# Second network in scaled float16 pairs, with its partial sums kept in three PSUM banks

## The chip, the cores and the metric

The kernel runs on one core of one Trainium2 chip. The metric is the device time of the program in microseconds, taken as the median of three runs of it. The profile is of one execution of the same program.

## What is computed

Three stages follow each other. First comes an attention over 2 x 8 heads, 768 positions and 64 values per head, in which each query sees only the keys that fall into the same hash bucket (six sign bits). Its output is laid out as 1536 tokens of 512 values. The first network and the second network then work on the tokens:

```python
def _moe_ref(x, w_in, w_out):            # 512 -> 2048 -> 512
    h = x @ w_in
    g = h - np.tanh(h)
    return (g @ w_out).astype(np.float32)

def _moe2_ref(x, domain_probs, w1, w2):  # 4 experts, 512 -> 1024 -> 512
    p = domain_probs / (domain_probs.sum(-1, keepdims=True) + 1e-09)
    out = np.zeros((N, D), dtype=np.float32)
    for e in range(E):
        h = np.maximum(x @ w1[e], 0.0)
        out += p[:, e:e + 1] * (h @ w2[e])
    return out.astype(np.float32)
```

The weights of the first network come in as float64, all the rest as float32.

## The kernel before

All work is put down as a list of operations (`Plan.add`, line 130), each with a priority, the engines that may do it with a planned cost, what it reads and writes, and the buffers that it uses. `Plan.order` (line 155) then plays this list through on the planned costs. At each moment it takes, for each free engine, the operation with the lowest sum of priority and planned wait, and gives out buffers as they come free. The order that results is the order in which every engine, and SP's queue of DMA issues, gets its instructions. Nothing is reordered later: an instruction that waits holds up what stands behind it on its engine. A class of buffers may receive its members late in the plan (`gives_later`, `hand`), when what used the same memory has been planned.

Precision is kept by pairs: an operand is written as a high part and the remainder, and a product is made by three matmuls, high by high, high by remainder and remainder by high. In the attention the pairs are float16. In both networks they are float32r.

*First network.* The tokens are worked on in three blocks (c = 0, 1, 2) of 512. `network_up` (line 804) makes 16 blocks of hidden units, `network_down` (line 822) adds them into four banks of PSUM. At the end four copies on ScalarE (line 1118) put a block's result, transposed, back into `xs[c]`. For block 2 these copies wait until everything that batch 0 still reads from the old buffers is done (`sums[0]`).

*Between the networks.* The second network uses Strassen's scheme in Winograd's form: seven products in place of eight. The tokens make two batches (b = 0, 1) of 768, and each is cut into halves of 384 tokens and halves of the 512 inputs. `moving(b)` (line 860) makes seven operands for the batch, three of them halves of the input themselves, four of them differences, and cuts each into a pair: the high part on ScalarE (line 322), the remainder on VectorE or GpSimd (line 325). `moving(0)` has a priority of 540, `moving(1)` of 734; the down groups of block 2 have 580 to 730.

*Second network.* There are 16 blocks u of hidden units (4 experts, 4 blocks of 256 units each). `stationary(u)` (line 913) loads the weights, makes four sums of quarters of the first matrix (line 927, VectorE or GpSimd), and cuts seven stationary operands and the rows of the second matrix into pairs. `step2(u, b)` (line 945) is one step. It has seven products of six matmuls of 384 columns (line 958), each into a bank of its own. Seven additions on VectorE (`plus`, line 969) and one copy on ScalarE combine them into four results of the hidden layer. `hidden` makes a pair of each: a relu on ScalarE (line 978) and the remainder on VectorE (line 979). Then come six groups, one for each 128 tokens, of six matmuls of 512 columns (`down3`, line 1013), the down groups. VectorE multiplies each by the expert's weight and adds it to the output in `xs` (lines 1021 and 1023). Two banks serve the down groups and six the products. The priorities run 20 units per step, and the down groups of a step lie beside the products of the next. The first writing of the output (u = 0) waits until both batches are cut, since the output takes the place of the cut tokens.

The last step's outputs go to HBM from SP's queue.

Of the kernel before, what the change touches and what calls it, by code (L numbers as in the profile page):

```python
# [16 lines left out]
P = 128  # L17
# [31 lines left out]
NST = 3  # L49
NRQ = 2  # L50
# [31 lines left out]


class Same(Slot):
    def __init__(self, of):
        super().__init__()
        self.of = of

    @property
    def tile(self):  # L90
        return self.of.tile

    @tile.setter
    def tile(self, t):
        pass
# [150 lines left out]
def attn_moe_kernel(ctx: ExitStack, tc: tile.TileContext, qk, v, proj, ident, wa, wb, dp, out):  # L246
# [34 lines left out]
    xs = [xo.tile([P, 4, DM], F32, tag="xo", name=f"xs{c}") for c in range(NC)]  # L281

# [576 lines left out]

    def moving(b, p):  # L860

        bo = [("bo%d" % b, o) for o in range(7)]

        def xat(kh, c, a, n):
            return xs[c][:, 2 * kh : 2 * kh + 2, a : a + n]

        def x2(kh, *cs):
            return [("x2", c, db) for c in cs for db in (2 * kh, 2 * kh + 1)]

        def cut_(o, src, i, j, r, use, p):  # L870

            n = 2 * (j - i)
            hi, lo = (lambda: pl[bo[o]][:, :, 0, i:j]), (lambda: pl[bo[o]][:, :, 1, i:j])
            h32 = lambda: hi().bitcast(F32)
            k = ("part", *bo[o], i)
            sums[b].append(add(p, {AC: (0.05 + n * 0.92e-3, act_copy(hi, src))}, r, [(k, "hi")], [bo[o], *use]))
            sums[b].append(both(
                p + 0.1, sub(nc.vector, lo, src, h32), sub(nc.gpsimd, lo, src, h32), n, [*r, (k, "hi")], [(k, "lo")], [bo[o], *use]
            ))
# [33 lines left out]
    def stationary(u, p):  # L913
# [15 lines left out]
        for m, (o, n, src, r) in enumerate((  # L929
# [5 lines left out]
            h32 = lambda hi=hi: hi().bitcast(F32)  # L935
            k = ("parts", u, m)
            use = [ao, *w, *([sx] if m == 2 else [])]
            add(p + 3 + m, {AC: (0.05 + n * 0.19, act_copy(hi, src))}, r, [(k, "hi")], use)
            both(p + 3.1 + m, sub(nc.vector, lo, src, h32), sub(nc.gpsimd, lo, src, h32), 256 * n, [*r, (k, "hi")], [(k, "lo")], use)
        for i in range(2):  # L940
            w2, v_ = ("wr", u, i, 1), ("w2", u, i)
            dma(p + 2, lambda w2=w2: pl[w2], lambda i=i: wb[e * NF2 + 2 * j + i, :, 1], w=[w2], lat=1.1)
            split(p + 8 + i, lambda v_=v_: pl[v_], lambda w2=w2: pl[w2], [w2], ("w2k", u, i), [v_])

    def step2(u, b, p, q):

        e, j = divmod(u, NF2 // 2)
        ch = {o: ("ch", u, b, o) for o in range(7)}
        ao = ("ao", u)
        bank = lambda o: pl[ch[o]][:, 0:HN]  # L950

        def product(pm, a, o):
            def f():
                n = 0
                for k in range(2):
                    hi, lo = (pl[ao][:, a, i, k * P : k * P + P] for i in range(2))
                    for x, i in ((hi, 0), (hi, 1), (lo, 0)):
                        nc.tensor.matmul(bank(o), x, pl["bo%d" % b, o][:, k, i, :], start=(n == 0), stop=(n == 5))  # L958
                        n += 1

            m = (0, 0, 1, 2, 2, 2, 2)[a]
            return add(p + pm, {TE: (1.04, f)}, [(("parts", u, m), i) for i in ("hi", "lo")] + ready_[b][o], [ch[o]], [ao])

        rs = [("rs", u, b, n) for n in range(2)]

        def plus(pm, o, n, to=None):

            dst = (lambda: bank(o)) if to is None else (lambda: pl[rs[to]][:, 0:HN])
            add(p + pm, {VE: (0.465, lambda: nc.vector.tensor_tensor(out=dst(), in0=bank(o), in1=pl[rs[n]][:, 0:HN], op=ALU.add))},  # L969
                [ch[o], rs[n]], [ch[o] if to is None else rs[to]])  # L970
# [4 lines left out]
        def hidden(pm, o, i, s):  # L975
            hi, lo = (lambda x=x: pl[hb[i]][:, x, s * HN : s * HN + HN] for x in range(2))
            k, key = ("hk", u, b, i, s), ch[o]
            add(p + pm, {AC: (0.37, lambda: nc.scalar.activation(hi(), bank(o), AF.Relu))}, [key], [(k, "hi")], [hb[i]])  # L978
            add(p + pm + 0.1, {VE: (0.465, lambda: nc.vector.scalar_tensor_tensor(
                out=lo(), in0=bank(o), scalar=0.0, in1=hi().bitcast(F32), op0=ALU.max, op1=ALU.subtract  # L980
            ))}, [key, (k, "hi")], [(k, "lo")], [hb[i]])
# [7 lines left out]
        product(2, 4, 4)  # L989
        plus(2.5, 4, 0, 0)  # L990
        product(4, 5, 5)
        plus(4.5, 5, 0, 1)
        product(6, 3, 3)
        plus(6.5, 3, 0, 0)
        plus(6.6, 3, 1)
        hidden(6.7, 3, 1, 1)
        product(8, 2, 6)
        plus(8.5, 6, 1)
        hidden(8.6, 6, 1, 0)
        product(10, 6, 2)  # L1000
        plus(10.5, 2, 0)
        hidden(10.6, 2, 0, 1)
        for t in range(2 * HN // P):
# [13 lines left out]
            add(q + (2, 5, 7, 8, 11, 12)[t], {TE: (1.362, down3)},  # L1017
# [8 lines left out]
            add(q + (2, 5, 7, 8, 11, 12)[t] + 0.5, {VE: (0.66, f)}, [dn, ("pw",), ("o", tb)], [("o", tb)], after=sums[0] + sums[1] if u == 0 else ())  # L1026
# [84 lines left out]
    for c in range(NC):  # L1111
# [4 lines left out]
        for db in range(4):  # L1116
# [41 lines left out]
    new = {"fo": NF1 - 3, "fo2": 3, "xp1": KB4, "raw": 2, "wd": 2, "bo0": 2}  # L1158
# [7 lines left out]
    def switch():  # L1166
# [3 lines left out]
        def space(name, words, kind=F32):  # L1170
# [30 lines left out]
    def stationaries():  # L1201
        t = space("fa", 14 * CH, F32R)
        return [part(t, i * 7 * CH, 7 * CH).rearrange("p (o i n) -> p o i n", o=7, i=2) for i in range(2)]

    def hiddens(t, n):
        return [part(t, MV * i, MV).rearrange("p (i n) -> p i n", i=2) for i in range(n)]

    gives_later("bo0", 3, lambda: made["bo0a"], ups1)
    for n in ("rw", "rq"):
        gives_later("bo0", 1, lambda n=n: movers(space(n, 2 * 2 * CH, F32R), 0, 1), raw_)  # L1210
    gives_later("bo1", 4, lambda: movers(space("fb", 13 * CH, F32R), 0, 4), net)
    gives_later("bo1", 1, lambda: movers(space("hp2", 4 * CH, F32R), 0, 1), net)
    gives_later("bo1", 2, lambda: movers(xa_t, 0, 2), ups2)
    gives_later("ao", 2, stationaries, ups2)
    gives_later("sx", 1, lambda: [fa2_t.rearrange("p (o n) -> p o n", o=4)], ups2)
    gives_later("wr", 2, lambda: made["wr"], ups2)
    gives_later("hb", 3, lambda: hiddens(space("tp", NTH * CH, F32R), 3), net)
    gives_later("hb", 1, lambda: hiddens(hp_t, 1), net)
    gives_later("w2", 2, lambda: made["w2"], net)
# [4 lines left out]
    outs2 = those("fo2")  # L1224
    for n in range(3):
        hand("fo2", n, "rs", False, outs2)
    for n in range(2):
        hand("wu", n, "w2", False, ups2)
# [59 lines left out]
```

## Time and profile before

| what | us |
|---|---|
| median of three runs | 983.17 |
| lowest and highest run | 982.15, 983.32 |
| span of the profiled execution | 978.8 |
| TensorE busy | 964.1 |
| VectorE busy | 754.3 |
| ScalarE busy | 438.8 |
| GpSimd busy | 294.2 |

The span reaches from the first to the last instruction of the profiled execution, whose own time is not listed apart from its span; the runs' times hold some microseconds more, outside it. The profile calls TensorE's matmuls PE and its weight loads PEld, VectorE DVE, ScalarE ACT, GpSimd POOL and SyncE SP; line numbers (L958) are those of the kernel before. A tile's name stands for the memory that an operation writes or reads, by the pool that held it first: in the second network `fa` is the stationary operands, `ab`, `fb`, `xa`, `rw`, `rq` and `hp` are operands of the products, and `st`, `sf`, `po` are banks of PSUM. Matmuls are pipelined, so a matmul's own duration is longer than the time from its start to the next one's; prices of matmuls are taken from start to start.

### The profile page before, as it was taken

What the parts mean: (1) busy time and instruction counts of PE and PEld (TensorE: products, weight loads), DVE (VectorE), ACT (ScalarE), POOL (GpSimd) and SP (SyncE); (2) the same over time, 40 slices, a digit from 0 to 9 for tenths busy, and PEclk for the clock granted to TensorE, in tenths of its full rate; (3) what the DMA queues carried; (4) which work ended last, traced back from release to release, by engine and by line L of the source; (5) the groups of instructions that cost most, each with busy time, mean ns of one, the idle gap of its engine ahead of it and who ended that gap; (6) DMA issues with size and microseconds to landing.
All of it is one profiled execution on the core that took longest, in us unless ns stands there. A gap on an engine that the chain in (4) does not pass through costs nothing.

```text
span 978.8 us, 17209 instructions
## 1 busy us (share of the span) xinstructions
PE 964.1 (99%) x6508; PEld 804.3 (82%) x6508; DVE 754.3 (77%) x1324; ACT 438.8 (45%) x908; POOL 294.2 (30%) x313
## 2 busy tenths in 40 slices
PE   8999999999999999999999999999999999999998
PEld 4767667777788888887889989898989989898997
DVE  8989998888887565578787777777777777777665
ACT  7899989888544433353522222222132322222210
POOL 4687887785533010044421100111001100111000
PEclk9999999999999999999999999999999999999999
DMA  5533342222531000001101101010101101011003
GB/s 169 163 86 87 87 128 84 80 85 70 170 127 46 1 1 1 0 1 44 33 33 44 44 22 44 22 44 24 42 22 44 44 22 44 22 43 41 4 1 130
DMA packets 32010, 53.78 MB, mean 55 GB/s; under 512 B 6135, under 2 KB 11063, under 8 KB 31927
## 3 DMA queue, kind: packets, MB, share of 16 engines
q1 hardware_dynamic: 31926, 52.68, 17.4%
q8 instruction: 51, 0.84, 0.4%
q14 instruction: 33, 0.26, 0.1%
HBM read 43.18 MB, written 3.15 MB: 47 GB/s over the span
## 4 chain that ended last, share of the span: by engine, by line
PE 88%; DVE 5%; DMA 2%; SPq 1%; issue 1%; ACT 1%; POOL 1%; DVEq 0%; POOLq 0%; ACTq 0%
PE st L1013 27%; PE sf L958 11%; PE po L958 8%; PE sf L317 6%; PE sf L304 6%; PE st L304 6%; PE st L958 4%; PE po L317 4%; PE st L317 2%; PE st L651 2%; PE sf L567 2%; PE st L656 2%; DVE mx L573 2%; SPq L393 1%; DMA qk<-bt 1%
## 5 line engine op out<-in xcount | busy, mean ns | idle before, releaser
L1013 PE MATMUL st<-w,tp 128*128 128x512 f32 x864 | 227.8, 393 | 0.0
L1023 DVE SCALAR_TENSOR_TENSOR xs<-st,pw,xs 128x512 f32<-128x512 f32 x180 | 135.0, 750 | 79.2 <-PE st L1013 78.9
L1013 PEld LDWEIGHTS st<-w,tp 128*128 128x128 f32 x864 | 159.9, 188 | 24.0
L325 POOL TENSOR_TENSOR ph<-p,ph 128x384 f16<-128x384 f32 x132 | 126.3, 976 | 48.6 <-ACT ph L662 28.3
L573 DVE TENSOR_REDUCE mx<-sf 128x1 f32<-128x384 f32 x192 | 98.3, 549 | 15.7 <-PE sf L567 14.6
L927 POOL TENSOR_TENSOR fa<-ab 128x256 f32<-128x256 f32 x18 | 14.1, 787 | 299.0 <-DMA ab<-wb 275.6
L662 ACT ACTIVATE ph<-st 128x384 f16<-128x384 f32 x192 | 92.2, 505 | 0.5 <-PE st L656 0.4
L1013 PE MATMUL st<-w,hp 128*128 128x512 f32 x288 | 81.6, 392 | 0.0
L304 PE MATMUL sf<-hp,w 128*128 128x512 f32 x288 | 74.7, 392 | 0.9 <-DVE hp L325 0.7
L662 ACT ACTIVATE p<-st 128x384 f32<-128x384 f32 x144 | 71.7, 498 | 6.8 <-PE st L656 5.2
L304 PE MATMUL st<-hp,w 128*128 128x512 f32 x288 | 73.5, 389 | 0.0
L978 ACT ACTIVATE tp<-sf 128x384 fp32r<-128x384 f32 x56 | 27.3, 489 | 94.5 <-DVE sf L969 93.5
L317 PE MATMUL sf<-xa,w 128*128 128x512 f32 x240 | 65.2, 410 | 1.6 <-DVE den L730 1.0
L1013 PEld LDWEIGHTS st<-w,hp 128*128 128x128 f32 x288 | 54.0, 188 | 12.5
L304 PEld LDWEIGHTS sf<-hp,w 128*128 128x128 f32 x288 | 53.5, 188 | 13.0 <-DVE hp L325 1.4
L651 PE MATMUL st<-qk 97*128 97x384 f16 x192 | 62.9, 328 | 1.0 <-ACT ph L662 0.7
L304 PEld LDWEIGHTS st<-hp,w 128*128 128x128 f32 x288 | 54.1, 188 | 11.4
L656 PE MATMUL st<-qk 128*128 128x384 f16 x192 | 62.7, 326 | 0.0
L707 PE MATMUL po<-v,ph 128*128 128x64 f16 x576 | 62.0, 195 | 0.0
L706 PE MATMUL po<-v,ph 128*128 128x65 f16 x576 | 62.0, 192 | 0.0
L708 PE MATMUL po<-v,ph 128*128 128x65 f16 x576 | 61.7, 191 | 0.0
L567 PE MATMUL sf<-qk 96*128 96x384 f16 x192 | 56.2, 327 | 4.2 <-DMA qk<-bt 3.4
(227 smaller groups left out, 2038.2 us busy)
## 6 DMA issues: line engine op xcount, KB each, us to landing
ab<-wb SPq DMA_DIRECT2D x64, 256.0 KB
rw<-wa SPq DMA_DIRECT2D x48, 256.0 KB
r<-qk SPq DMA_DIRECT2D x15, 384.0 KB
qk<-qk SPq DMA_DIRECT2D x58, 96.0 KB
rq<-wa SPq DMA_DIRECT2D x16, 256.0 KB
vr<-v SPq DMA_DIRECT2D x8, 384.0 KB
out<-xs SPq DMA_DIRECT2D x12, 256.0 KB
qk<-bt SPq DMA_DIRECT2D x56, 9.0 KB
```

The lines of the kernel that those rows point to most:

```text
L304: nc.tensor.matmul(acc, a, g[:, i, :], start=(first and n == 0), stop=(last and n == 2))
L317: nc.tensor.matmul(ph, a, xt[kb][:, i, :], start=(m == 0), stop=(m == n - 1))
L325: return lambda: eng.tensor_tensor(out=dst(), in0=a(), in1=b(), op=ALU.subtract)
L567: nc.tensor.matmul(pl[ps][:, 0:384], t[0:96, QA, qt * P : qt * P + P], t[0:96, KB, j * 384 : j * 384 + 384], start=True, stop=True,)
L573: nc.vector.tensor_reduce(out=pl["mx", h][:, qt, j : j + 1], in_=pl[ps][:, 0:384], axis=AX.X, op=ALU.max)
L651: nc.tensor.matmul(ps[j][:, 0:384], t[0:97, KB, kt * P : kt * P + P], t[0:97, QA, j * 384 : j * 384 + 384], start=True, stop=False,)
L656: nc.tensor.matmul(ps[j][:, 0:384], t[:, KC, kt * P : kt * P + P], t[:, QC, j * 384 : j * 384 + 384], start=False, stop=True,)
L662: nc.scalar.activation(o.rearrange("p (a b) -> p a b", a=2)[:, js[0]], pl[st][:, 0:384], AF.Exp, scale=1.0 / (8.0 * SC * SC),)
L706: nc.tensor.matmul(o[:, c : c + D + 1], hi, vt[:, kt, 0 : D + 1], start=(kt == 0 and qt == 0), stop=False)
L958: nc.tensor.matmul(bank(o), x, pl["bo%d" % b, o][:, k, i, :], start=(n == 0), stop=(n == 5))
L1013: nc.tensor.matmul(pl[dn], x, w[:, y, :], start=(n == 0), stop=(n == 5))
L1023: f = lambda dn=dn, o=o, sc=sc: nc.vector.scalar_tensor_tensor(out=o(), in0=pl[dn], scalar=sc, in1=o(), op0=ALU.mult, op1=ALU.add)
```

## The change

The operands of the second network become float16 pairs in place of float32r pairs.

- *Scales.* The weights are multiplied by 64 and 256 as they are cut. The tokens of a batch are multiplied by a power of two that is worked out on the chip from the batch's largest absolute value: `scaling(b)`, from maxima over each quarter of each block. The inverse is multiplied into the experts' weights.
- *Remainders.* The remainder of an operand is one scalar_tensor_tensor on VectorE (source times scale, minus high part). GpSimd no longer takes remainders in the second network; it may still take differences, sums of quarters and the new addition in SBUF.
- *Three banks.* The seven products go to three banks X, Y and Z. A product that continues a sum is accumulated by the matmuls onto what the bank holds (`start` only for the first product of a bank); between two products the bank's sum is copied out by ScalarE (`keep`), where it is wanted, or gets a kept sum added by VectorE (`plus`, in place).
- *Order.* `moving(0)` gets a priority of 740 in place of 540. The planner's costs of a product and of a down group are set to 0.99 and 1.3 (from 1.04 and 1.362).
- *Buffers.* The halved operands are laid out anew; the stationary operands, the pairs of the second matrix, the hidden pairs and the raw weights get more buffers (2 to 4, 4 to 8, 4 to 6, 2 to 6).

The core of the diff:

```diff
+    def scaling(b, p):
+
+        g, e = gm[:, 2 * b : 2 * b + 1], gme[:, 2 * b : 2 * b + 1]
+        t, ebits = gm[:, 2 * b + 1 : 2 * b + 2], gme[:, 2 * b + 1 : 2 * b + 2]
+        up_, down_ = scl[:, 2 * b : 2 * b + 1], scl[:, 2 * b + 1 : 2 * b + 2]
+        k, bank = ("gm", b), ("ch", "gm", b)
+        small = lambda f, r, w: add(p, {VE: (0.12, f)}, r, w)
+        small(lambda: nc.vector.tensor_reduce(out=t, in_=mxa[:, 4 * b : 4 * b + 8], axis=AX.X, op=ALU.max),
+            [("mxa", c, db) for c in (b, b + 1) for db in range(4)], [k])
+        add(p, {TE: (0.11, lambda: nc.tensor.transpose(pl[bank][:, 0:P], t.to_broadcast([P, P]), id32))}, [k, ("id32",)], [bank])
+        add(p, {VE: (0.25, lambda: nc.vector.tensor_reduce(out=g, in_=pl[bank][:, 0:P], axis=AX.X, op=ALU.max))}, [bank], [k])
...
+        scaling(b, p - 0.5)
+        up_ = scl[:, 2 * b : 2 * b + 1]
...
-            sums[b].append(add(p, {AC: (0.05 + n * 0.92e-3, act_copy(hi, src))}, r, [(k, "hi")], [bo[o], *use]))
-            sums[b].append(both(
-                p + 0.1, sub(nc.vector, lo, src, h32), sub(nc.gpsimd, lo, src, h32), n, [*r, (k, "hi")], [(k, "lo")], [bo[o], *use]
+            sums[b].append(add(p, {AC: (0.05 + n * 0.92e-3, act_copy(hi, src, scale=up_))}, r, [(k, "hi")], [bo[o], *use]))
+            sums[b].append(add(p + 0.1, {VE: (0.07 + n * 1.04e-3, lambda: nc.vector.scalar_tensor_tensor(
+                out=lo(), in0=src(), scalar=up_, in1=hi(), op0=ALU.mult, op1=ALU.subtract
...
-        product(0, 0, 0)
-        add(p + 0.5, {AC: (0.37, act_copy(lambda: pl[rs[0]][:, 0:HN], lambda: bank(0)))}, [ch[0]], [rs[0]])
-        product(1, 1, 1)
-        plus(1.5, 1, 0)
-        hidden(1.6, 1, 0, 0)
...
+        product(0, 0, 0, X, True)
+        keep(0.5, X, 0)
+        product(1, 4, 4, Y, True)
+        plus(1.5, Y, 0)
+        keep(1.6, Y, 1)
+        product(2, 3, 3, Z, True)
+        keep(2.5, Z, 3)
+        product(4, 1, 1, X)
+        hidden(4.5, lambda: bank(X), X, 0, 0)
+        plus(4.6, Z, 1)
+        product(6, 5, 5, Y)
+        keep(6.5, Y, 2)
+        product(8, 6, 2, Z)
+        hidden(8.5, lambda: bank(Z), Z, 0, 1)
+        product(10, 2, 6, Y)
+        hidden(10.5, lambda: bank(Y), Y, 1, 0)
+        both(8.6 + p, *(lambda eng=eng: eng.tensor_tensor(out=kept(2), in0=kept(2), in1=kept(3), op=ALU.add)
+            for eng in (nc.vector, nc.gpsimd)), HN, [rs[2], rs[3]], [rs[2]])
+        hidden(8.8, lambda: kept(2), rs[2], 1, 1, False)
...
+            add(down_at(c, NF1) - 7.9, {VE: (0.6, lambda c=c, db=db: nc.vector.tensor_reduce(
+                out=mxa[:, 4 * c + db : 4 * c + db + 1], in_=xs[c][:, db, :], axis=AX.X, op=ALU.max, apply_absolute_value=True
+            ))}, [("x2", c, db)], [("mxa", c, db)])
...
-            moving(0, down_at(c, NF1))
+            moving(0, down_at(c, NF1) + 200)
```

## Rows read from the trace of the kernel before

**Rows 1.** The page: busy time by engine, and the granted clock by slices.

```profile
PE 964.1 (99%) x6508; PEld 804.3 (82%) x6508; DVE 754.3 (77%) x1324; ACT 438.8 (45%) x908; POOL 294.2 (30%) x313
...
PEclk9999999999999999999999999999999999999999
```

**Rows 2.** The chain that ended last, in time: start us, us, what.

```profile
332.36 2.72 PE st L317 x12
...
526.14 2.76 PE st L1013 x12
...
948.42 2.76 PE st L1013 x12
```

**Rows 3.** Window over 27 steps: us, busy time by engine (instructions), clock, DMA.

```profile
526.14:948.42 422.28, 422.28 (x2107) 380.04 (x2107) 314.48 (x524) 104.95 (x198) 37.18 (x49) 1.00 0.10 32
```

**Rows 4.** Timeline of TensorE in the second network: start us, us, what.

```profile
520.07 1.21 PE L958 MATMUL po<-fb,fa 128*128 128x384 f32 x6
521.11 1.55 PE L1013 MATMUL st<-w,tp 128*128 128x512 f32 x6
522.50 1.21 PE L958 MATMUL po<-fb,fa 128*128 128x384 f32 x6
```

**Rows 5.** Timeline of TensorE in the attention, six starts in a row.

```profile
60.25 0.33 PE L567 MATMUL sf<-qk 96*128 96x384 f16 x1
...
61.07 0.49 PE L567 MATMUL sf<-qk 96*128 96x384 f16 x2
```

**Rows 6.** Timeline of TensorE in the kernel's first microseconds.

```profile
6.71 1.37 PE L1084 MATMUL po<-warm 128*128 128x256 f16 x11
```

**Rows 7.** Groups of instructions by line and form: busy us, mean ns | idle before.

```profile
L573 DVE TENSOR_REDUCE mx<-sf 128x1 f32<-128x384 f32 x192 | 98.3, 549 | 15.7 <-PE sf L567 14.6
...
L927 POOL TENSOR_TENSOR fa<-fa,ab 128x256 f32<-128x256 f32 x16 | 13.0, 810 | 1.5 <-DVE fa L927 0.4
...
L969 DVE TENSOR_TENSOR sf<-sf,fb 128x384 f32<-128x384 f32 x68 | 38.0, 560 | 12.9 <-PE sf L958 12.9
...
L1084 PE MATMUL po<-warm 128*128 128x256 f16 x90 | 16.3, 275 | 0.1
...
L435 DVE SCALAR_TENSOR_TENSOR qk<-r,qk 128x768 f16<-128x768 f32 x15 | 15.7, 1051 | 0.0
...
L322 ACT ACTIVATE fb<-sf 128x384 f32<-128x384 f32 x14 | 6.9, 493 | 21.0 <-PE sf L958 21.0
```

**Rows 8.** Windows before and at the seam of the two networks, columns as above.

```profile
478.00:500.00 22.00, 21.59 (x110) 19.42 (x110) 20.97 (x33) 13.50 (x26) 16.12 (x13) 1.00 0.14 48
...
434.00:478.00 44.00, 43.29 (x196) 36.09 (x195) 34.33 (x48) 16.91 (x29) 17.77 (x14) 1.00 0.13 37
```

**Rows 9.** Window of the instructions that touch xs alone.

```profile
420.00:440.00 20.00, 0.00 (x0) 0.00 (x0) 6.21 (x6) 6.29 (x10) 9.20 (x6) 1.00 0.00 0
```

**Rows 10.** Groups of GpSimd and of VectorE from 478 to 500 us.

```profile
L325 POOL TENSOR_TENSOR w<-ab,w 128x512 fp32r<-128x512 f32 x2 | 3.3, 1656 | 0.0
L325 POOL TENSOR_TENSOR fa<-fa,fa 128x1024 fp32r<-128x1024 f32 x1 | 2.4, 2410 | 0.5 <-ACT fa L322 0.5
L325 POOL TENSOR_TENSOR fa<-ab,fa 128x512 fp32r<-128x512 f32 (+1 forms) x2 | 2.0, 1014 | 0.0
...
L325 POOL TENSOR_TENSOR xa<-xs,xa 128x256 fp32r<-128x256 f32 x1 | 1.1, 1117 | 0.7 <-ACT xa L322 0.7
...
L325 DVE TENSOR_TENSOR fb<-xs,fb 128x768 fp32r<-128x768 f32 x4 | 5.1, 1283 | 0.0
```

**Rows 11.** Timeline at the seam: a first cut and the last remainder of batch 1.

```profile
479.90 0.42 ACT L322 ACTIVATE xa<-xs 128x256 fp32r<-128x256 f32 x1
...
490.66 0.94 DVE L325 TENSOR_TENSOR hp<-xs,hp 128x768 fp32r<-128x768 f32 x1
```

**Rows 12.** Timeline of the last steps: a product's copy, and the group behind the product.

```profile
952.08 1.20 PE L958 MATMUL sf<-xa,fa 128*128 128x384 f32 x6
952.28 0.49 ACT L322 ACTIVATE fb<-po 128x384 f32<-128x384 f32 x1 [2.60 <-PE po L958]
```

More of the change, by code (lines that the diff above doesn't have):

```diff
@@ L49 @@
 NST = 3
+WS1, WS2, XS = 64.0, 256.0, 16.0
+EXPO = 0x7F800000
+TINY = 2.0**-90
 NRQ = 2
@@ L858, in both @@
         return add(p, how, r, w, use, port=not psum)
+    def scaling(b, p):
[8 more added lines that the diff above has]
+        add(p, {VE: (0.25, lambda: nc.vector.tensor_reduce(out=g, in_=pl[bank][:, 0:P], axis=AX.X, op=ALU.max))}, [bank], [k])
+        small(lambda: nc.vector.tensor_scalar(out=g, in0=g, scalar1=TINY, scalar2=None, op0=ALU.max), [k], [k])
+        small(lambda: nc.vector.tensor_scalar(
+            out=e, in0=g.bitcast(U32), scalar1=EXPO, scalar2=EXPO, op0=ALU.bitwise_and, op1=ALU.bitwise_xor
+        ), [k], [("ge", b)])
+        small(lambda: nc.vector.tensor_scalar(out=up_, in0=e.bitcast(F32), scalar1=XS, scalar2=None, op0=ALU.mult), [("ge", b)], [("scl", b)])
+        small(lambda: nc.vector.tensor_scalar(
+            out=ebits, in0=g.bitcast(U32), scalar1=EXPO, scalar2=None, op0=ALU.bitwise_and
+        ), [k], [("gi", b)])
+        small(lambda: nc.vector.tensor_scalar(
+            out=down_, in0=ebits.bitcast(F32), scalar1=0.5 / (XS * WS1 * WS2), scalar2=None, op0=ALU.mult
+        ), [("gi", b)], [("inv", b)])
+        tb = slice(b * NB, b * NB + NB)
+        add(p + 3, {VE: (0.12, lambda: nc.vector.tensor_scalar(
+            out=pw[:, tb, :], in0=pw[:, tb, :], scalar1=down_, scalar2=None, op0=ALU.mult
+        ))}, [("inv", b), ("pw",)], [("pws", b)])
     def moving(b, p):
+        scaling(b, p - 0.5)
+        up_ = scl[:, 2 * b : 2 * b + 1]
         bo = [("bo%d" % b, o) for o in range(7)]
@@ L934, in stationary @@
             hi, lo = (lambda o=o, n=n: pl[ao][:, o : o + n, 0]), (lambda o=o, n=n: pl[ao][:, o : o + n, 1])
[L935 to L939, printed above, removed]
+            scaled(p + 3 + m, hi, lo, src, WS1, 256 * n, r, ("parts", u, m), [ao, *w, *([sx] if m == 2 else [])])
         for i in range(2):
@@ L942, in stationary, with scaled, product @@
             dma(p + 2, lambda w2=w2: pl[w2], lambda i=i: wb[e * NF2 + 2 * j + i, :, 1], w=[w2], lat=1.1)
-            split(p + 8 + i, lambda v_=v_: pl[v_], lambda w2=w2: pl[w2], [w2], ("w2k", u, i), [v_])
+            hi, lo = (lambda v_=v_: pl[v_][:, 0]), (lambda v_=v_: pl[v_][:, 1])
+            scaled(p + 8 + i, hi, lo, lambda w2=w2: pl[w2], WS2, CH, [w2], ("w2k", u, i), [v_, w2])
+    def scaled(p, hi, lo, src, by, n, r, k, use):
+        add(p, {AC: (0.05 + n * 0.92e-3, act_copy(hi, src, scale=by))}, r, [(k, "hi")], use)
+        add(p + 0.1, {VE: (0.07 + n * 1.04e-3, lambda: nc.vector.scalar_tensor_tensor(
+            out=lo(), in0=src(), scalar=by, in1=hi(), op0=ALU.mult, op1=ALU.subtract
+        ))}, [*r, (k, "hi")], [(k, "lo")], use, port=True)
     def step2(u, b, p, q):
         e, j = divmod(u, NF2 // 2)
-        ch = {o: ("ch", u, b, o) for o in range(7)}
         ao = ("ao", u)
-        bank = lambda o: pl[ch[o]][:, 0:HN]
-        def product(pm, a, o):
+        X, Y, Z = (("ch", u, b, o) for o in range(3))
+        bank = lambda x: pl[x][:, 0:HN]
+        rs = [("rs", u, b, n) for n in range(4)]
+        kept = lambda n: pl[rs[n]]
+        def product(pm, a, o, x, first=False):
             def f():
@@ L956, in f @@
                     hi, lo = (pl[ao][:, a, i, k * P : k * P + P] for i in range(2))
-                    for x, i in ((hi, 0), (hi, 1), (lo, 0)):
-                        nc.tensor.matmul(bank(o), x, pl["bo%d" % b, o][:, k, i, :], start=(n == 0), stop=(n == 5))
+                    for s, i in ((hi, 0), (hi, 1), (lo, 0)):
+                        nc.tensor.matmul(
+                            bank(x), s, pl["bo%d" % b, o][:, k, i, :], start=(first and n == 0), stop=(n == 5), skip_group_check=True
+                        )
@@ L959, in f @@
                         n += 1
             m = (0, 0, 1, 2, 2, 2, 2)[a]
[L962 to L970, printed above, removed]
+            add(p + pm, {TE: (0.99, f)}, [(("parts", u, m), i) for i in ("hi", "lo")] + ready_[b][o] + ([] if first else [x]), [x], [ao])
@@ L972, in step2, with keep, plus, hidden @@
+        def keep(pm, x, n):
+            add(p + pm, {AC: (0.37, act_copy(lambda: kept(n), lambda: bank(x)))}, [x], [rs[n]])
+        def plus(pm, x, n):
+            add(p + pm, {VE: (0.465, lambda: nc.vector.tensor_tensor(out=bank(x), in0=bank(x), in1=kept(n), op=ALU.add))}, [x, rs[n]], [x])
         hb = [("hb", u, b, i) for i in range(2)]
         hk = {}
-        def hidden(pm, o, i, s):
+        def hidden(pm, src, key, i, s, psum=True):
             hi, lo = (lambda x=x: pl[hb[i]][:, x, s * HN : s * HN + HN] for x in range(2))
-            k, key = ("hk", u, b, i, s), ch[o]
-            add(p + pm, {AC: (0.37, lambda: nc.scalar.activation(hi(), bank(o), AF.Relu))}, [key], [(k, "hi")], [hb[i]])
+            k = ("hk", u, b, i, s)
+            add(p + pm, {AC: (0.37, lambda: nc.scalar.activation(hi(), src(), AF.Relu))}, [key], [(k, "hi")], [hb[i]])
@@ L979, in hidden @@
             add(p + pm + 0.1, {VE: (0.465, lambda: nc.vector.scalar_tensor_tensor(
-                out=lo(), in0=bank(o), scalar=0.0, in1=hi().bitcast(F32), op0=ALU.max, op1=ALU.subtract
-            ))}, [key, (k, "hi")], [(k, "lo")], [hb[i]])
+                out=lo(), in0=src(), scalar=0.0, in1=hi(), op0=ALU.max, op1=ALU.subtract
+            ))}, [key, (k, "hi")], [(k, "lo")], [hb[i]], port=not psum)
             hk[i, s] = [(k, "hi"), (k, "lo")]
-        product(0, 0, 0)
-        add(p + 0.5, {AC: (0.37, act_copy(lambda: pl[rs[0]][:, 0:HN], lambda: bank(0)))}, [ch[0]], [rs[0]])
@@ L1025, in step2 @@
                 )
-            add(q + (2, 5, 7, 8, 11, 12)[t] + 0.5, {VE: (0.66, f)}, [dn, ("pw",), ("o", tb)], [("o", tb)], after=sums[0] + sums[1] if u == 0 else ())
+            add(q + (2, 5, 7, 8, 11, 12)[t] + 0.5, {VE: (0.66, f)}, [dn, ("pws", b), ("o", tb)], [("o", tb)], after=sums[0] + sums[1] if u == 0 else ())
             if u == NU - 1:
@@ L1199, in gives_later @@
         add(1e4, {None: (0.0, f)}, gives=give(cls, *slots), after=after)
[L1201 to L1210, printed above, removed]
@@ L1219, in attn_moe_kernel, with cut16, shared @@
-    gives_later("w2", 2, lambda: made["w2"], net)
+    def cut16(name, words, n, shape, count, at=0):
+        t = space(name, words, F16)
+        return [part(t, at + n * i, n).rearrange(*shape[:1], **shape[1]) for i in range(count)]
+    mover = ("p (k i n) -> p k i n", dict(k=2, i=2))
+    gives_later("bo0", 2, lambda: cut16("rw", 8 * CH, MV, mover, 2), raw_)
+    gives_later("bo1", 2, lambda: cut16("rq", 8 * CH, MV, mover, 2), raw_)
+    late = {}
+    def shared():
+        late["bo"] = cut16("ab", KB4 * 4 * CH, MV, mover, 5)
+        return late["bo"][:1]
@@ new lines, in attn_moe_kernel, with extra @@
+    gives_later("bo0", 1, shared, ups1)
+    gives_later("bo1", 4, lambda: late["bo"][1:], ups1)
+    gives_later("ao", 4, lambda: cut16("fa", 28 * CH, 7 * CH, ("p (o i n) -> p o i n", dict(o=7, i=2)), 4), ups2)
+    def extra():
+        t = space("xa", KB4 * 2 * CH)
+        late.update(sx=part(t, 0, 2 * CH).rearrange("p (o n) -> p o n", o=4), wr=singles(t, 2 * CH, 4))
+        late["bo1"] = movers(t.bitcast(F16), 12 * CH, 1)
+        return [late["sx"], fa2_t.rearrange("p (o n) -> p o n", o=4)]
@@ new lines, in attn_moe_kernel, with kept_slots @@
+    gives_later("sx", 2, extra, ups2)
+    gives_later("bo1", 1, lambda: late["bo1"], ups2)
+    gives_later("wr", 6, lambda: made["wr"] + late["wr"], ups2)
+    halves = ("p (i n) -> p i n", dict(i=2))
+    def kept_slots():
+        t = space("fb", 13 * CH)
+        return [part(t, HN * i, HN) for i in range(12)]
+    gives_later("hb", 6, lambda: cut16("tp", 2 * NTH * CH, MV, halves, 6), net)
+    gives_later("w2", 4, lambda: cut16("hp", 8 * CH, 2 * CH, halves, 4), net)
+    gives_later("w2", 4, lambda: cut16("hp2", 8 * CH, 2 * CH, halves, 4), net)
@@ L1220, in attn_moe_kernel @@
+    gives_later("rs", 12, kept_slots, net)
     for b, c, after in ((0, 2, turns[2]), (1, 0, sums[0])):
@@ L1223, in attn_moe_kernel @@
         ], after)
[L1224 to L1228, printed above, removed]
     for n in range(4):
```

51 lines of the change are left out of this document (11 added, 40 removed).

## The prediction

> **What bounds the kernel now.** I began with the busy shares: TensorE is busy for 964.1 us of a span of 978.8 us, 99%, and the granted clock stands at nine tenths or more in every slice, the 2.4 GHz level [rows 1]. A busy TensorE can still be waiting inside its shares, so the second view was the chain of work that ended last, in order of time. There one pattern of the second network returns: the group of twelve matmuls of line 1013 that starts at 526.14 us comes again at 948.42 us, 27 steps later [rows 2]. One step (a block of 256 hidden units for one batch) thus takes 422.28 / 27 = 15.64 us, and 32 such steps make 500 us, half of the kernel. Third, the same stretch cut out as a window: TensorE 422.28 us busy of 422.28, VectorE 314.48, ScalarE 104.95, GpSimd 37.18 [rows 3]. So in the second network nothing is waited for: the step costs what its matmuls cost, one behind the other, and VectorE has a quarter of the time free. That one fact decides what a change of the data type can be worth.
>
> The step's price by its matmuls: six matmuls of 384 columns take 1.04 us from their start to the next group's, 0.1733 us each, and six of 512 columns take 1.39 us, 0.2317 us each [rows 4]. 42 of the first and 36 of the second make 7.28 + 8.34 = 15.62 us, the period found above.
>
> **The change, part by part.**
>
> *The type of the matmuls.* All 78 matmuls of a step stay, with float16 operands. The trace shows float16 at the same clock in the attention stage: five matmuls of 384 columns, each with weights of its own, start 0.82 us apart in all, 0.164 to 0.165 us each [rows 5]. For 512 columns there is no such row. The nearest are float16 matmuls of 256 columns, eleven in 1.37 us [rows 6]; less the last one's own 0.275 us [rows 7] ten starts share 1.095 us, 0.11 us each, so two of them are 0.22 us, and 384 columns scaled by 4/3 give 0.219 us. I take 0.219. As bounds: a float32r matmul of 512 columns in the first network takes 2.72 / 12 = 0.227 us [rows 2], which float16 should not exceed; on the other side 0.164 us plus 128 columns at the 2.4 GHz level is 0.217 us. The new step is 42 x 0.165 + 36 x 0.219 = 6.93 + 7.88 = 14.81 us. Saved are 0.83 us a step, 26 us in 32 steps; 17 us by the upper bound (step 15.10) and 30 us by the lower one (14.70).
>
> The Trainium skill (TensorE: Matmul & The Clock Gate, "Back-to-back issue gap") gives a warm matmul N/2.4 + 2.5 ns, so 162.5 and 215.8 ns; by it, as an estimate, the step would be 14.6 us, the gain 33 us and the time 953 us. The rows at 384 columns read 2 ns more than it, and I go by the rows.
>
> *Three banks.* A product's evacuation changes from seven additions on VectorE and one copy on ScalarE to two additions on VectorE, four copies (keep) on ScalarE, and one addition in SBUF that VectorE or GpSimd may do. With 0.56 us for an addition and 0.49 us for a copy [rows 7], VectorE loses 5 x 0.56 = 2.8 us a step, less 0.55 if it does the SBUF one, and ScalarE gains 3 x 0.49 = 1.5 us: from 314.48 / 27 = 11.6 to some 9.5 us and from 3.9 to 5.4 us, both under 14.8. The splits of weights lose GpSimd as a helper; the larger remainders there ran on VectorE before, so this adds only small GpSimd splits, under 0.5 us a step. None of this sets the step; its cover is the 14.8 us of matmuls, and without it the longest engine would still be VectorE at about 10 us. What is new on the path is an order: a product that adds into bank X, Y or Z has to wait until the sum before it was copied out. That is the rival below; I price it at nothing, since six down groups of the step before (7.9 us) and the other banks' products stand between.
>
> *Scaling, and batch 0 moved back.* Twelve maxima over 128x512 and a short chain for each batch come new. For a maximum the nearest rows are 549 ns for 384 columns [rows 7], so about 0.7 us; those of the first block are off the path. The chain (a reduction, a TensorE transpose, a second reduction, five tiny operations, each passed between engines) is some 3 us of latency. For batch 0 the cutting is put back by 200 of the planner's units, behind everything that the first network still wants of VectorE and ScalarE. It has to end by the last down group of that network, because the copies of block 2 wait for it. Today it takes 6.21 us of VectorE and 9.20 us of GpSimd between 420 and 440 us [rows 9]. With the remainders on VectorE alone (seven of 768 elements at 1.05 us [rows 7], 7.4 us), the differences still shared (some 3 us of VectorE) and four maxima (2.8 us) it wants some 13 us of VectorE, where 6.21 are spent now; from 434 to 478 us VectorE is free for 9.7 us of 44 [rows 8]. So it fits, and I charge nothing. The moved operations issue no DMAs, so SP's queue keeps its order; on GpSimd their differences now come behind or beside its sums of quarters for the first blocks, 0.8 us each [rows 7], of which no one is in need before the products.
>
> *The seam at 478 us.* Here the cover is thin. From 478 to 500 us VectorE is busy for 20.97 of 22 us [rows 8]. GpSimd's remainders in that stretch (3.3, 2.4, 2.0 and 1.1 us [rows 10]) come to VectorE, about 4.1 us at its prices; four maxima (2.8 us) and the small chain (1.2 us) are added, and of the additions five a step go, in 22 / 15.64 = 1.4 steps seven of 0.56 us, with the new ones in SBUF 3.6 us. That is 25.5 us of VectorE work for 22 us: I charge 3.5 us of stall. Bounds: nothing, if products of later blocks of batch 0 fill in; 10 us, if TensorE has only the first block of batch 0 (7 us of products, and two down groups before both banks for them are full, since the output may be written only when batch 1 is cut) against a cutting that now lasts from 479.9 to 491.6 us [rows 11], plus 3 us for the scale and some 4 us of VectorE overload.
>
> *The end.* The last outputs follow the last down groups as now, by the same operations and stores, and the last groups stand behind each other without a product between. Nothing for that.
>
> **Sum.** -26.4 + 3.5 = -22.9 us. The profiled execution spans 978.8 us and the runs' median is 983.17 us (982.15 to 983.32), 4.4 us of which lie outside the span; I assume that these stay. 983.2 - 22.9 gives 960 us.
>
> **The rivals.**
>
> *A longer seam.* If VectorE falls behind by the whole upper bound at 478 us, the stall is 10 to 15 us: 967 to 972 us. For it: VectorE's 95% there [rows 8]. Against: an operation that reads SBUF takes longer there while GpSimd runs (1283 ns for four remainders, 0.94 us for the last, behind GpSimd's work [rows 10, 11]), and GpSimd will run less. Still faster.
>
> *The type is not what costs.* The 174 ns could come from the surroundings of the second network (its engines, its banks) and not from float32r; then 384 columns stay at 173 ns, nothing is saved, and the seam's 3.5 us remain: 987 us. For it: the same 512 columns cost 0.227 us in one network and 0.232 us in the other [rows 2, 4], so surroundings count for something, 2%. Against: 0.164 us in the attention stage, where every engine is busier. Here the Trainium skill speaks against the change (the same page, "Weight-path perf modes"): the array takes one element per cell and cycle whatever its width. It says so of two other types; the rows of this trace show 0.173 us against 0.164 us and don't agree for float32r.
>
> *The banks' hand-overs (the one that is slower).* Where a product stands right behind the one whose sum it adds to, TensorE waits: a copy of 0.49 us, begun 0.2 us after the product gave way to the next [rows 12], with as much behind it, is 0.9 us, an addition and a copy 1.65 us. A step has one of the second kind and about three of the first: 4.2 us bare. In 32 steps that is 134 us, against 26 us won, so it decides as soon as a fifth of it is uncovered; at 30% it is 40 us and the time 1000 us. For it: an order written ahead with planned costs can be wrong for a new pattern, and a stall in it recurs 32 times. Against: the present step has as many hand-overs (product, addition, relu, remainder) and no idle time in 27 steps [rows 3], and six banks still hold two steps.
>
> **How the numbers follow.** Two microseconds (0.2%) is about what a measurement of this kernel can tell from no change. The forecast gets 0.80, the longer seam 0.10, the useless type 0.04, the hand-overs 0.06. Faster by over 0.2% takes the first two, a little of what is left ends within 0.2%: 0.90, 0.02, 0.08. The range runs from a gain of 30 us without a stall (953) to the longer seam (972), widened by 1 us below for the clean pitch that no row shows.
>
> **What would show it.** Right: the period of the down groups falls from 15.64 to about 14.8 us, a product's six matmuls take 0.99 us from start to start and a down group's 1.31 us, TensorE without gaps from 500 us on, and a gap of a few us between the first network's last matmul and the second's steady state, with VectorE full there. Wrong: a period near 15.6 us without gaps (the type), matmul groups at 0.99 us with gaps behind ScalarE copies or VectorE additions in every step (the banks), or 10 us and more of idle TensorE at the seam.

## The result: 951.16 us, and the profile after

The changed kernel takes 951.16 us (median of four runs, 949.67 to 952.74) beside 982.66 us for the kernel before (981.61 to 983.32): a ratio of 0.9681, with a 95% interval of 0.9667 to 0.9694. It is 31.5 us faster. The prediction, 960 us with a range of 952 to 972, had the direction, but took the gain for 23 us; the median lies 0.8 us below the range. The spans of the two profiled executions differ by less, 978.8 and 951.0 us: the profiled execution of the kernel before was some 2.6 us shorter than its median run (the listed runs have only some 1.8 of the 4.4 us outside their spans), and that of the changed kernel reaches the first network 3.6 us later (145.08 for 141.52 us). So the whole is judged by the medians, and the profiles are used stage by stage.

The page of the changed kernel, busy time by engine and the clock's slices:

```profile
PE 933.6 (98%) x6510; PEld 598.5 (63%) x6510; DVE 714.0 (75%) x1244; ACT 486.4 (51%) x1011; POOL 269.3 (28%) x286
...
PEclk9999999999999999999999999999999999999999
```

Against [rows 1] TensorE's busy time falls by 30.5 us and its weight loads' by 206 us, VectorE falls by 40 us and ScalarE rises by 48 us. TensorE remains the engine that sets the time. The chain that ended last, in time (start us, us, what), shows the same recurring pattern as [rows 2]:

```profile
538.23 2.59 PE st L1040 x12
...
705.90 1.95 PE sf L985 x12
...
932.29 2.59 PE st L1040 x12
```

The twelve matmuls of two down groups (now line 1040) come at 538.23 and, 27 steps later, at 932.29 us. The step is 394.06 / 27 = 14.595 us in place of 15.640. The same rows give the prices: 1.95 / 12 = 0.1625 us for 384 columns (0.1733 before [rows 4]) and 2.59 / 12 = 0.2158 us for 512 (0.2317 before). 42 of the one and 36 of the other make 14.59 us: nothing else is in the step. Over 32 steps the 1.045 us less are 33.4 us.

The seam gives a little back. Windows of the changed kernel (us, busy time of PE, PEld, DVE, ACT, POOL, then the clock, the DMA share and GB/s), and one of the kernel before:

```profile
480.00:490.00 10.00, 8.84 (x52) 4.69 (x51) 9.97 (x23) 9.86 (x22) 4.42 (x6) 1.00 0.31 99
490.00:500.00 10.00, 9.50 (x55) 5.30 (x56) 9.90 (x13) 9.75 (x18) 5.60 (x6) 1.00 0.02 7
500.00:520.00 20.00, 19.17 (x101) 9.73 (x100) 19.64 (x32) 7.87 (x17) 6.33 (x6) 1.00 0.19 64
420.00:520.00 100.00, 97.51 (x474) 67.53 (x474) 87.75 (x142) 56.90 (x103) 32.35 (x30) 1.00 0.14 45
```

```profile
420.00:520.00 100.00, 98.88 (x466) 85.06 (x465) 82.06 (x119) 41.92 (x74) 42.88 (x34) 1.00 0.11 32
```

VectorE is full from 480 to 520 us and TensorE idles for 2.49 us in the 100 us about the seam; before, it was 1.12 us (0.71 from 445 to 450 and 0.41 from 480 to 485). Of the 2.49 us, 1.9 end with an operation of VectorE and 0.6 with a copy on ScalarE, which is nearly full too from 480 to 500 us (19.6 of 20 us). So the account is -33.4 + 1.4 = -32.0 us, against 31.5 measured.

### The profile page after: what moved, and what is told of

It reads as the page before. It is cut to its first block, busy times and chain, and to the rows that moved or that the text cites. A ratio compares the mean times of both kernels' runs of the same rounds, so it can differ in the third digit from the quotient of the medians.

```text
span 951.0 us, 17022 instructions
## 1 busy us (share of the span) xinstructions
PE 933.6 (98%) x6510; PEld 598.5 (63%) x6510; DVE 714.0 (75%) x1244; ACT 486.4 (51%) x1011; POOL 269.3 (28%) x286
## 4 chain that ended last, share of the span: by engine, by line
PE 86%; DVE 7%; DMA 2%; ACT 1%; issue 1%; POOL 1%; SPq 1%; DVEq 0%; POOLq 0%; ACTq 0%
PE st L1040 26%; PE sf L985 10%; PE po L985 7%; PE sf L311 6%; PE sf L298 6%; PE st L298 6%; PE po L311 4%; PE st L985 4%; PE st L645 3%; PE sf L561 2%; PE st L650 2%; PE st L311 2%; DVE mx L567 2%; PE po L701 1%; PE po L700 1%
## 5 line engine op out<-in xcount | busy, mean ns | idle before, releaser
L1040 PE MATMUL st<-hp,tp 128*128 128x512 f16 x1152 | 268.7, 379 | 1.4 <-DVE xs L1048 0.8
L985 PEld LDWEIGHTS <-fa 128*128 128x128 f16 x1344 | 131.2, 98 | 101.5 <-issue 2.8
L1040 PEld LDWEIGHTS <-tp 128*128 128x128 f16 x1152 | 112.6, 98 | 125.2 <-DVE tp L1006 1.1
L1050 DVE SCALAR_TENSOR_TENSOR xs<-st,pw,xs 128x512 f32<-128x512 f32 x180 | 135.0, 750 | 30.5 <-PE st L1040 24.7
L316 ACT ACTIVATE fb<-sf 128x384 f32<-128x384 f32 x63 | 30.8, 489 | 65.9 <-PE sf L985 51.3
L316 ACT ACTIVATE w<-fb 128x512 fp32r<-128x512 f32 x42 | 26.6, 633 | 63.0 <-PE st L298 50.8
L700 PEld LDWEIGHTS <-ph 128*128 128x128 f16 x576 | 53.7, 96 | 5.6 <-issue 0.3
```

The source lines that it names most:

```text
L700: nc.tensor.matmul(o[:, c : c + D + 1], hi, vt[:, kt, 0 : D + 1], start=(kt == 0 and qt == 0), stop=False)
L985: nc.tensor.matmul(bank(x), s, pl["bo%d" % b, o][:, k, i, :], start=(first and n == 0), stop=(n == 5), skip_group_check=True)
L1040: nc.tensor.matmul(pl[dn], x, w[:, y, :], start=(n == 0), stop=(n == 5))
L1050: f = lambda dn=dn, o=o, sc=sc: nc.vector.scalar_tensor_tensor(out=o(), in0=pl[dn], scalar=sc, in1=o(), op0=ALU.mult, op1=ALU.add)
```

## The experiments

**The price of a matmul by itself.**

```diff
-    (the whole kernel)
+    for i in range(24):
+        nc.tensor.matmul(bk[2][:, 0:384], hi(w16, i), m16[:, 0:384], start=(i % 6 == 0), stop=(i % 6 == 5))
+    (the same for 256 and 512 columns, for float32r, and for six of 384 and six of 512 in turn)
```

> This kernel leaves the whole computation out: it runs rows of 24 matmuls alone, of 256, 384 and 512 columns, in float16 and in float32r, then groups of six of 384 and six of 512 in turn in either type, then float16 ones of 384 columns that each begin and end a sum in another bank, with 97 rows, and with a VectorE read behind each. Theory: a matmul costs its columns at 2.4 GHz plus a fixed part that depends on the type: float16 0.109, 0.1625 and 0.216 us from start to start, float32r about 0.120, 0.173 and 0.227 us (13 ns more than the columns), and in turn of 384 and 512 the float32r ones of 512 rise to 0.23 us as in the second network of the kernel before. Rival: float32r costs in proportion, 8.4% more than the columns: 0.116, 0.1735 and 0.231 us. The 0.165 us that the prediction took from the attention should come back in one of the last three rows, which tells what made it; if all three read 0.1625, its cause lies in the attention stage.

The timeline of TensorE (start us, us, what):

```profile
14.69 2.78 PE L256 MATMUL bk<-m,w 128*128 128x256 f16 x24
17.31 4.06 PE L258 MATMUL bk<-m,w 128*128 128x384 f16 x24
21.21 5.34 PE L260 MATMUL bk<-m,w 128*128 128x512 f16 x24
26.20 3.22 PE L262 MATMUL bk<-m,w 128*128 128x256 f32 x24
29.26 4.33 PE L264 MATMUL bk<-m,w 128*128 128x384 f32 x24
33.43 5.64 PE L266 MATMUL bk<-m,w 128*128 128x512 f32 x24
38.91 1.15 PE L269 MATMUL bk<-m,w 128*128 128x384 f16 x6
...
44.44 1.46 PE L271 MATMUL bk<-m,w 128*128 128x512 f16 x6
45.73 1.14 PE L269 MATMUL bk<-m,w 128*128 128x384 f16 x6
...
50.44 1.21 PE L274 MATMUL bk<-m,w 128*128 128x384 f32 x6
51.49 1.55 PE L276 MATMUL bk<-m,w 128*128 128x512 f32 x6
52.88 1.21 PE L274 MATMUL bk<-m,w 128*128 128x384 f32 x6
...
57.74 4.08 PE L278 MATMUL bk<-m,w 128*128 128x384 f16 x24
61.66 4.07 PE L280 MATMUL bk<-m,w 97*128 97x384 f16 x24
65.56 5.64 PE L282 MATMUL bk<-m,w 128*128 128x384 f16 x24
```

Starts are to be read, not durations. Float16: (17.31 - 14.69) / 24 = 0.109 us for 256 columns, (21.21 - 17.31) / 24 = 0.1625 for 384, and (45.73 - 44.44) / 6 = 0.215 for 512. Float32r: (33.43 - 29.26) / 24 = 0.174 for 384 and (38.91 - 33.43) / 24 = 0.228 for 512. These two hold some slower starts at the head of their rows, and where a row of one type follows one of the other (at 26.20 us) the difference of the rows' starts gives no clean price. Start by start, float16 of 512 columns keeps 0.2158 us, and float32r settles at 0.120, 0.1733 and 0.2267 us for 256, 384 and 512 columns. Each 128 columns more thus add 0.0533 us in both types. So float32r does not cost in proportion; what is left beside the columns is a fixed 13 ns per matmul, where float16 has 2.5. The rival falls. In turn of 384 and 512, float32r takes 1.05 and 1.39 us per six, as in the kernel before, and float16 stays at its price.

The three rows meant for the 0.165 us of the attention didn't bring it back: 3.92 / 24 = 0.163 us with a bank for each, 3.90 / 24 = 0.1625 with 97 rows, and with a VectorE read behind each the first nine run at the same pace before the reads hold them up. The trace of the kernel before shows what these rows lack. The four matmuls between the two rows of [rows 5] are:

```profile
60.41 0.33 PE L651 MATMUL st<-qk 97*128 97x384 f16 x1
60.58 0.33 PE L656 MATMUL st<-qk 128*128 128x384 f16 x1
60.74 0.33 PE L651 MATMUL st<-qk 97*128 97x384 f16 x1
60.91 0.33 PE L656 MATMUL st<-qk 128*128 128x384 f16 x1
```

From one to the next the number of rows changes, between 96, 97 and 128. Throughout the attention, before and after the change, such a matmul takes 0.164 to 0.168 us from its start to the next one's, while one of 96 rows behind another of 96 rows takes 0.160 to 0.163. In the isolated rows, too, the first matmul with 97 rows and the first with 128 rows behind these take 0.167 us, and those that follow 0.162. So the 2.5 ns go with a change of the number of rows; that this is their cause is read from the traces, and no run was made that alternates the rows alone.

**Seven banks again, in float16.**

```diff
-        product(0, 0, 0, X, True)
-        keep(0.5, X, 0)
...
+        product(0, 0, 0)
+        add(p + 0.5, {AC: (0.37, act_copy(lambda: kept(0), lambda: bank(0)))}, [ch[0]], [rs[0]])
+        product(1, 1, 1)
+        plus(1.5, 1, 0)
...
```

> Float16 and scales as changed, but the seven products go to a bank each again, with seven additions on VectorE and one copy on ScalarE per step. Theory (TensorE alone sets the step, the three banks win nothing by themselves): the step stays at 14.60 us and the time within 3 us of the changed kernel, 949 to 955 us; VectorE rises to some 12 us a step. Rival (the relief of VectorE is part of the gain): gaps in every step, 0.2 us or more of them, 958 us or more.

954.46 us, a ratio of 0.9709 (0.9696 to 0.9722) to the kernel before, within the theory's 949 to 955 us. Windows of this kernel, and one of the changed kernel with it:

```profile
420.00:520.00 100.00, 93.61 (x455) 64.60 (x454) 89.42 (x153) 50.59 (x88) 26.80 (x25) 1.00 0.14 44
480.00:490.00 10.00, 6.13 (x36) 3.50 (x36) 10.00 (x24) 9.19 (x16) 4.36 (x3) 1.00 0.18 52
490.00:500.00 10.00, 8.23 (x46) 4.23 (x44) 10.00 (x19) 3.58 (x7) 2.20 (x4) 1.00 0.15 52
600.00:900.00 300.00, 300.00 (x1606) 156.86 (x1604) 237.82 (x405) 76.56 (x146) 10.20 (x14) 1.00 0.08 25
```

```profile
600.00:900.00 300.00, 300.00 (x1606) 156.91 (x1604) 202.58 (x323) 104.73 (x207) 10.76 (x14) 1.00 0.08 25
```

In 300 us of steady steps both run 1606 matmuls and TensorE has no gap, though VectorE is at 79% with seven banks and at 68% with three. The relief of VectorE buys nothing there. It buys something only where VectorE is full: at the seam TensorE idles 6.4 us with seven banks and 2.5 with three, about the 3 us between the two medians. Of the 6.4 us, 3.6 end with an operation of VectorE and 2.8 with a copy on ScalarE, and the order of the products goes back too, so that VectorE's additions alone make the difference is argued and not shown.

**Batch 0 cut early again, and half-way.**

```diff
-            moving(0, down_at(c, NF1) + 200)
+            moving(0, down_at(c, NF1))
```

> As changed, but the cutting of batch 0 keeps the priority it had before (540 in place of 740). Theory: the place of this work moves only what lies about the seam of the two networks, 0 to 4 us slower (951 to 955 us), by idle TensorE between 420 and 480 us. Rival (putting it back is what kept the seam short): idle time of 5 us or more there, 957 us or more.

964.59 us, a ratio of 0.9804 (0.9791 to 0.9817): 13 us slower than the changed kernel. The theory's 0 to 4 us fell and the rival held. The timeline of TensorE, and that of VectorE, in this kernel:

```profile
443.25 0.39 PE L298 MATMUL sf<-hp,w 128*128 128x512 f32 x1
455.22 2.50 PE L298 MATMUL sf<-hp,w 128*128 128x512 f32 x5 [11.58 <-DVE hp L319]
```

```profile
441.95 5.36 DVE L899 SCALAR_TENSOR_TENSOR ac<-xs,scl,ac 128x768 f16<-128x768 f32 x5
447.23 1.01 DVE L899 SCALAR_TENSOR_TENSOR rw<-xs,scl,rw 128x768 f16<-128x768 f32 x1
...
453.09 1.47 DVE L899 SCALAR_TENSOR_TENSOR ab<-xs,scl,ab 128x768 f16<-128x768 f32 x1
454.48 0.68 DVE L319 TENSOR_TENSOR hp<-hp,hp 128x512 fp32r<-128x512 f32 x1
```

TensorE stands for 11.58 us in one piece. It waits for the remainder of the first network's hidden values (`hp`, line 319), which VectorE writes only after it has gone through the remainders of batch 0 (line 899, eight operations of 9.2 us in all) and some other work between them, from 441.95 to 454.56 us. Before the change GpSimd shared the work on batch 0 ([rows 9]: 9.20 us on it); now the remainders are VectorE's alone. The window from 440 to 460 us of this kernel shows a second cost: the mean granted clock is 0.66 there. It fell while TensorE stood and is 0.50, the 1.2 GHz level, from 446 to 458 us, so the five matmuls from 455.22 us take 2.50 us, where five at the 2.4 GHz level (from 468.91 us) take 1.32:

```profile
440.00:460.00 20.00, 8.42 (x29) 6.47 (x29) 18.20 (x21) 11.14 (x17) 10.78 (x10) 0.66 0.07 26
```

A second kernel put the cutting back by half as much:

```diff
-            moving(0, down_at(c, NF1) + 200)
+            moving(0, down_at(c, NF1) + 100)
```

> As changed (first network float32r), but the cutting of batch 0 is put back by 100 units in place of 200 (priority 640, in the middle of the down groups of block 2). Theory (VectorE does the whole cut of 12 us in one piece as soon as its priority comes before the hidden pairs that the next down group waits for, and TensorE idles for it): about as long as with the old priority or a part of it, 955 to 965 us, with one gap of TensorE of several us between 440 and 470 us. Rival (only the old place is bad): 949 to 953 us.

951.08 us, a ratio of 0.9683 (0.9656 to 0.9709). The rival held: of the three places only the old one is bad. Here the remainders stand between other work of VectorE (line 899, from 448.77 to 461.13 us), and TensorE idles 2.98 us of the 100 about the seam. The mechanism of the theory shows in small, since 2.3 of these 2.98 us are waits for a remainder `hp`; but from 480 to 500 us, where the changed kernel idles 1.66 us, this one idles nothing:

```profile
448.77 3.93 DVE L899 SCALAR_TENSOR_TENSOR ac<-xs,scl,ac 128x768 f16<-128x768 f32 x5
453.82 1.01 DVE L899 SCALAR_TENSOR_TENSOR rw<-xs,scl,rw 128x768 f16<-128x768 f32 x1
458.24 1.02 DVE L899 SCALAR_TENSOR_TENSOR rw<-xs,scl,rw 128x768 f16<-128x768 f32 x1
```

With the priority of 640 the plan puts remainders of the first network before and between those of the cut; with 540 nearly the whole cut came ahead of the one remainder that TensorE waited for.

**Without maxima and scale chain.**

```diff
-        small(lambda: nc.vector.tensor_reduce(out=t, in_=mxa[:, 4 * b : 4 * b + 8], axis=AX.X, op=ALU.max),
...
+        small(lambda: nc.vector.memset(up_, 64.0), [], [("scl", b)])
+        small(lambda: nc.vector.memset(down_, 1.0 / (64.0 * WS1 * WS2)), [], [("inv", b)])
```

> As changed, but the twelve maxima, the transpose and the small chain are left out: the tokens' scale is the constant 64, and the inverse goes into the experts' weights as before. Theory: the idle 2.5 us of TensorE between 480 and 520 us come from VectorE being full there, of which the maxima and the chain are some 4 us; without them 1 to 3 us of the time go, 948 to 950 us. Rival (the chain's latency holds the cutting of batch 1 and costs more than the idle time shows): 945 us or less. Rival (hidden): 951 us, unchanged.

952.48 us, a ratio of 0.9692 (0.9679 to 0.9705): no gain, as the second rival had it. From 480 to 520 us TensorE does idle less (1.39 in place of 2.49 us), but the plan came out in another order and lost 3.4 us between 420 and 460 us, where the changed kernel loses none:

```profile
420.00:440.00 20.00, 18.89 (x84) 15.35 (x83) 17.27 (x21) 10.33 (x17) 8.76 (x7) 1.00 0.16 53
440.00:460.00 20.00, 17.73 (x77) 13.98 (x76) 16.88 (x25) 9.45 (x16) 6.79 (x6) 1.00 0.09 27
```

So the run doesn't price the chain alone: what the lighter VectorE gave back at the seam (1.1 us) is less than what a change of the order can cost.

**Down groups in float32r again.**

```diff
-    gives_later("hb", 6, lambda: cut16("tp", 2 * NTH * CH, MV, halves, 6), net)
...
+    gives_later("hb", 3, lambda: cut32("tp", NTH * CH, MV, halves, 3), net)
...
```

> As changed, but the hidden pairs and the second matrix are float32r pairs again, so the 1152 matmuls of the down groups (512 columns) have their old type, and the 1344 of the products keep float16. Theory (the gain is a fixed part per matmul that float32r has over float16): each of the 1152 takes 0.227 to 0.232 us in place of 0.216, 13 to 18 us in all: 963 to 969 us, by a step of 15.0 to 15.16 us in place of 14.60 and no idle TensorE in it. Rival (banks, order or VectorE carry the gain): under 5 us, 956 us or less.

971.09 us, a ratio of 0.9885 (0.9870 to 0.9901). With the type, the planned cost of a down group and the smaller numbers of buffers for these operands go back too. The changed kernel, measured beside it:

> The changed kernel itself, beside the others on the same chip: 951 us, 949 to 953, a ratio to the kernel before of 0.967 to 0.969.

951.47 us, a ratio of 0.9690 (0.9665 to 0.9715). The chain of the kernel with float32r down groups:

```profile
543.88 2.77 PE st L1041 x12
...
937.87 2.77 PE st L1041 x12
```

26 steps in 393.99 us are 15.153 us each, 0.558 us more than with float16, 15.5 ns for each of the 36 matmuls: the float32r price comes back in full, and 32 steps make 17.9 of the 19.6 us. Most of the rest lies at the seam (3.3 us of idle TensorE from 460 to 500 us, 1.7 in the changed kernel beside it). The time is 2 us above the expected 963 to 969 us, which counted the steps alone.

**The first network in float16 as well.**

```diff
-        return p.tile([P, 2, CH], F32R, tag=tag, name=tag)
+        return p.tile([P, 2, CH], F16, tag=tag, name=tag)
...
-        gs = split(p - cut, lambda: pl[g], lambda: pl[th], [th], ("g", c, fb, "part"), [g], gp=False)
+        gs = split(p - cut, lambda: pl[g], lambda: pl[th], [th], ("g", c, fb, "part"), [g], gp=False, by=GS)
...
-                xs[c][:, db, :], pl["acc", c, db], AF.Copy
+                xs[c][:, db, :], pl["acc", c, db], AF.Copy, scale=1.0 / GS
```

> As changed, and the first network in float16 pairs too: its weights and tokens unscaled, its hidden values times 4096, taken back in the copies at its end; the same planned costs. Theory (10.8 ns of fixed part less for each matmul of 512 columns, and TensorE is the bound there too): 1152 matmuls make 12 us less, 938 to 941 us, and the groups of twelve of the up stage take 2.59 in place of 2.72 us. Rival (the first network is bound by VectorE and by the loads in its first half): 3 us or less, 948 us or more.

937.22 us (936.36 to 937.74), a ratio of 0.9537 (0.9524 to 0.9550) to the kernel before and 14.3 us less than the changed kernel measured beside it: the fastest of all, 0.8 us below the theory's 938 to 941 us. The rival fell. The chain has 2.59 us for twelve matmuls of the up stage, 2.72 before [rows 2]:

```profile
305.69 2.59 PE st L312 x12
```

1152 matmuls at 10.8 ns are 12.4 us of it. The last matmul of the first network starts at 463.63 us in place of 477.78, so the remaining 2 us lie ahead of the seam; their cause stays open. The same with one planned cost set to the new price:

> The kernel with the first network in float16 as well, with the planned cost of its down group lowered to what the matmuls take (0.648 in place of 0.68). Theory (TensorE is the bound up to the seam, so the plan's costs change only where the seam's idle time of 3.3 us falls): 935 to 939 us. Rival (a plan nearer to the chip removes the seam's idle time): 934 us or less.

938.00 us, a ratio of 0.9544 (0.9521 to 0.9567): no difference, as the theory had it.

## Why the prediction fell short

- **The bound** was read rightly. Before and after, TensorE has no gap in the steps, and the step is the sum of its 78 matmuls.
- **The term that failed** is the price of a float16 matmul, "42 x 0.165 + 36 x 0.219 = 14.81 us". It measured 42 x 0.1625 + 36 x 0.2158 = 14.59. Two and three nanoseconds look small, but there are 2496 of them: 6.9 us. The 0.165 us was a true row of another stage, whose matmuls change their number of rows from one to the next, as those of the second network do not. The 0.219 us came from doubling the 256 columns (0.1095 us, rounded up to 0.11) and from scaling up the 0.164, and both count the fixed part of a matmul more than once. The same row plus 256 columns at the 0.053 us per 128 that the prediction itself used gives 0.216.
- **The rule that the prediction set aside was right.** The Trainium skill (TensorE: Matmul & The Clock Gate, "Back-to-back issue gap") gives N/2.4 + 2.5 ns for the gap between isolated matmuls, so 162.5 and 215.8 ns. The isolated rows and the changed kernel agree with 0.1625 and 0.2158 us. By the rule the prediction's own sum gave 953 us.
- **The lower bound of the range** allowed 30 us of gain, from 0.164 and 0.217 us, "widened by 1 us for the clean pitch that no row shows". The clean pitch was worth 33.4 us, 3 more than that bound; 1.4 us of them went at the seam, and the 1 us of widening did not cover the rest.
- **The seam** was charged 3.5 us and cost 1.4 more than before. The mechanism is as named in the main (VectorE full from 480 to 520 us, and 1.9 of 2.5 us of waits end there), though ScalarE, full beside it, was not counted; "nothing, if products of later blocks of batch 0 fill in" was nearer. The 3 us for the scale in the upper bound stand on no row: from 481.63 to 488.84 us the chain of batch 1 took 7.2 us, with other work of VectorE between its parts. The 6.9 us of the matmuls and the 2.1 us here make 9.0 us; the prediction missed by 8.8.
- **Batch 0 put back** was costed at nothing, and cost nothing. What the prediction did not see is what it prevents: in the old place the remainders, now on VectorE alone, hold up TensorE for 11.6 us and the kernel is 13 us slower.
- **Three banks** were priced at nothing in the step, and that is what seven banks show (no gap either way); their 3 us are at the seam. The shift of work was read rightly: from 600 to 900 us VectorE has 9.9 us a step and ScalarE 5.1, for 9.5 and 5.4. The hand-overs, the slower rival, are covered in every step. (By its own terms a step has 4.3 us of them bare, not 4.2; nothing hangs on it.)
- **"The type is not what costs"** falls with the isolated rows: both types add 0.053 us for 128 columns more, and what differs is a fixed part per matmul. The rule of the Trainium skill named there, that the array takes one element per cell and cycle whatever its width (TensorE: Matmul & The Clock Gate, "Weight-path perf modes"), agrees with the columns' part.

## What to carry to other kernels

Where TensorE has no gap, price a change of type by the time from start to start of the very matmul, and take that from a clean run of it or from two lengths (a slope and a fixed part), not from another stage whose matmuls have other shapes around them: a few nanoseconds times thousands decided this forecast. An engine's relief bought nothing in the steps, where that engine had time to spare, so look first for the stretches where it is full. When a change takes a helper away from some work, look at what that work stands in front of on the engine that is left, and move it in the same step.

## What was not expected

- Float32r's fixed part of 13 ns per matmul, independent of its columns, against 2.5 ns for float16 (isolated, once settled: 0.1733 and 0.2267 us against 0.1625 and 0.2158). Where it comes from was not separated: a weight load also takes 188 ns in float32r (line 1013 before) and 98 ns in float16 (line 1040 after).
- A run of float32r matmuls of 512 columns starts slower than it goes on: in the isolated row the first ten take 0.231 us each and the others 0.2267. Six in turn with products take 1.39 us, 0.2317 each, with float32r products, and with float16 ones the pace is the same (2.77 / 12 = 0.231 in the kernel with float32r down groups), while a long run takes 2.72 / 12 = 0.2267. Groups of six and twelve hardly get to the faster pace; that is a third of what the down groups won.
- VectorE's remainder of 768 elements took 1.47 us where GpSimd was at work beside it and 1.01 us where it was not (both in the kernel with batch 0 cut early), so a price read while GpSimd runs, as the 1283 ns of [rows 10], is too high for work that is taken from GpSimd.
